# The RMS norms' sums over partitions: one full float32 matmul against two single-pass matmuls of a split operand

## The chip, the core and the metric

The program runs on one core of a Trainium2 chip. A core has five engines with a queue of their own each, worked off in order: TensorE (PE; its weight loads are listed apart as PEld), VectorE (DVE), ScalarE (ACT), GpSimd (POOL) and SyncE (SP), which here issues transfers. The metric is the device time of one execution in microseconds (us). Before the change the median of 3 runs is 1052.08 us (1051.79 to 1053.68).

## What is computed

```
attn = 1 / (1 + exp(-(q k^T / sqrt(D) - log(S))))        # 4 x 12 heads, S = 448, D = 64
x    = attn v, heads side by side                        # 1792 tokens x 768
rms  = sqrt(mean(x * x, axis=-1) + 1e-06)
xn   = x / rms * rms_g
h1   = silu(xn w_gate) * (xn w_val) w_out                # 768 -> 1536 -> 768
out  = ((h1 w1) * (h1 w2)) w3 w_out2                     # 768 -> 1024 -> 1024 -> 768
```

All in float32. The norm needs, for each token, the sum of squares over 768 features.

## The kernel before

Activations lie transposed: features on the 128 partitions, the S = 448 tokens of one batch along the row, so that a 768-wide x is six tiles of 128x448. The four batches b = 0 to 3 are worked off in turn.

Nearly all matmuls take float32 values that were split into two float32r parts, a high part (a copy rounded to float32r, on ScalarE or GpSimd) and a low part (value minus high part, on VectorE or GpSimd); `runs` (L351) multiplies high by high, high by low and low by high, three matmuls of 128x448 for each product. A matmul whose operands are plain float32 is carried out as two passes, which the trace lists as two matmuls of one instruction.

The sums of the norm: `take_out` (L504) squares each of a batch's six attention tiles (L516, L519) and GpSimd adds them up in `acc` (L520). `rms_norm` (L524) multiplies `acc` by a 128x128 tile of ones on TensorE (L529), in plain float32, which leaves the sum over the partitions in every partition of a PSUM tile; ScalarE takes it from there (v, L533), then come the root and its inverse (r, L535 to L544), and `load_x` (L552) multiplies x by r. `rms_norm` is called four times:

- norm 0 inside the attention of batches 0 and 1, between two pairs of heads (about 55 us into the span). VectorE and GpSimd decode and split weights there (`to_float`, L109, and `split_weight`, L132);
- norm 1 while the product of w3 and the last weight matrix is formed (`w3o_groups`, L944; about 99 us), when VectorE and GpSimd also split the x of batch 0;
- norm 2 in the stretch where the gate and value products of batches 0 and 1 (`a_group`, L855) run between the attention pairs of batches 2 and 3 (about 347 us);
- norm 3 after the last pair, between groups of the down product (`b_group`, L885; about 451 us).

From there to the end TensorE forms products of the Winograd kind without norms.

The scheduler of the tile layer sets the order on each engine from the program's order and its own costs, so the place of an instruction in an engine's queue can differ from its place in the code. Scratch tiles of 128x448 rotate through six buffers (`scratch`, L88); PSUM tiles named `psm` rotate through three (L94). Norms 0 and 1 put their sum in a `psm` tile, norms 2 and 3 in a tile `sn` of another pool.

Of the kernel before, what the change touches and what calls it, by code (L numbers as in the profile page):

```python
# [9 lines left out]
F32 = mybir.dt.float32  # L10
F32R = mybir.dt.float32r
U32 = mybir.dt.uint32
AF = mybir.ActivationFunctionType
ALU = mybir.AluOpType
PSUM = bass.MemoryType.PSUM

B, H, S, D = 4, 12, 448, 64
P = 128
# [27 lines left out]
def fused_kernel(ctx: ExitStack, tc: tile.TileContext, qkv, wg, wv, wo, w1, w2, w3, wo2, gam, out):  # L46
    nc = tc.nc

    def pool(name, side=None, space=None):
        kw = {}  # L50
        if side:
            kw["side"] = side
        if space is not None:
            kw["space"] = space
        return tc.alloc_tile_pool(name=name, bufs=1, **kw)

    cst = pool("cst", "left")
    r1a = pool("r1a", "left")
    scr = pool("scr", "left")
# [4 lines left out]
    ps_m = pool("ps_m", space=PSUM)  # L64
# [1 line left out]
    ps_sc = pool("ps_sc", space=PSUM)  # L66
    pools = {}

    ones = cst.tile([P, P], F32, name="ones")
    nc.vector.memset(ones, 1.0)  # L70
    g_sb = cst.tile([P, KD], F32, name="g_sb")
    bias_s = cst.tile([P, 1], F32, name="bias_s")
    nc.vector.memset(bias_s, -math.log(S))
# [5 lines left out]
    w3o = dram.tile([KF2, P, DM], F32, name="w3o")  # L79

    for _ in range(WARM):
        nc.tensor.matmul(ps_m.tile([P, 512], F32, tag="m", bufs=3, name="psm")[:, :P], ones, ones, start=True, stop=True)  # L82

    def parts(pool, tag, bufs, name, w=S, step=0):

# [2 lines left out]
    def scratch(name):  # L88
        return scr.tile([P, S], F32, tag="s", bufs=6, name=name)

    def held(name):
        return scr.tile([P, S], F32, tag="held", bufs=4, name=name)

    def psm():  # L94
        return ps_m.tile([P, 512], F32, tag="m", bufs=3, name="psm")
# [321 lines left out]
    raw, probs, av, acc = {}, {}, {}, {}  # L417
# [106 lines left out]
    def rms_norm(b, log=False):  # L524
        if b < 2:
            ps = psm()[:, :S]
        else:
            ps = ps_sc.tile([P, 2, 512], F32, tag="sc", bufs=2, name="sn")[:, 0, :S]
        nc.tensor.matmul(ps, ones, acc.pop(b), start=True, stop=True)  # L529
        v = scratch("v")  # L530
        r = rms[b] = held("r")
        t = scratch("t")
        nc.scalar.activation(v, ps, AF.Identity, bias=eps_b, scale=1.0 / DM)  # L533
        if log:
            nc.scalar.activation(t, v, AF.Ln)  # L535
            nc.scalar.activation(r, t, AF.Exp, scale=-0.5)
        else:
            nc.scalar.activation(t, v, AF.Sqrt)
            nc.vector.reciprocal(r, t)

        nc.vector.tensor_tensor(out=t, in0=r, in1=r, op=ALU.mult)
        nc.vector.tensor_tensor(out=t, in0=t, in1=v, op=ALU.mult)
        nc.vector.tensor_scalar(out=t, in0=t, scalar1=-0.5, scalar2=1.5, op0=ALU.mult, op1=ALU.add)
        nc.vector.tensor_tensor(out=r, in0=r, in1=t, op=ALU.mult)  # L544
# [355 lines left out]
    def b_units(g):  # L900
        for m in range(KD):
            for b in range(2):
                yield 6.8, (lambda m=m, b=b: b_group(g, m, b)), (i_b2 if g else i_b)[m][1]
# [23 lines left out]
    for i in range(NA + 1):  # L927
        visit(i, (0, NA, 2))
        with tc.issue_after(last_raw[0]):
            if i in DECODE:  # L930
                decode_wo2(DECODE[i])
                load_wo2(DECODE[i] + 2)
            if i in W3_AT:
                W.load_to(W3_AT[i] + 1)
                W.split_to(W3_AT[i] - 1)
        if i == NA - 2:
            load_pair(NA)
        if i == HP + 1:
            rms_norm(0)
        if i > HP + 1:  # L940
            split_x(0, i - HP - 2)
# [10 lines left out]
    split_x(0, KD)  # L952
    w3o_groups(1, (0,))
    rms_norm(1, True)
    w3o_groups(1, (1,))
    for k in range(KD):
# [32 lines left out]
    b = list(b_units(0))  # L989
    beside = a[half_a:] + b[:5]  # L990
    total, spent = sum(u[0] for u in beside), 0.0
    for j, u in enumerate(beside):
        spent += run(u, int(j >= half_a and j % 2 == 1))

        if 1 <= j <= 3:
            for c in ((0, 1), (2,), (3,))[j - 1]:
                scores(first, c)
            visits = list(range(first + 1, NP + 1))
        if j >= split_at and visits and visits[0] < NP and len(raw[visits[0]]) == 2:
            split_keys(visits[0])  # L1000
        while j > 3 and visits and NP + 1 - first - len(visits) < (NP + 1 - first) * (spent - 8.0) / (total - 8.0):
            visit(visits[0], (first, NP, 1))
            split_at = j + 1
            if visits.pop(0) == NA + HP:
                norm_at = j + 1
            if j >= half_a - 1 and visits and visits[0] < NP:
                split_keys(visits[0])
        if j == norm_at:
            rms_norm(2)
# [102 lines left out]
```

## Time and profile before

| | |
|---|---|
| median of 3 runs | 1052.08 us |
| the profiled execution | 1051.55 us |
| its span from first to last instruction | 1049.8 us |
| TensorE busy | 1043.9 us (99%) |
| VectorE busy | 805.5 us (77%) |
| ScalarE busy | 437.3 us (42%) |
| GpSimd busy | 380.6 us (36%) |

The span is the time between the first and the last instruction; 1.75 us of the execution lie around it. Busy shares alone don't tell what bounds a stage: the chain of waits, followed back from the last instruction, and the list of who waited for whom do. The start of a matmul in the trace is where it is issued; its length of some 0.37 us overlaps with that of its neighbours, so a matmul's price in a stream is the distance between starts, or a piece of the chain divided by its count.

### The profile page before, as it was taken

The page shows a single profiled execution, that of the slowest core. Times are in us where ns is not written, and L with a number is a line of the kernel's source. Part 1 is how long each engine was busy: PE and PEld are TensorE (multiplying, and loading weights), DVE is VectorE, ACT ScalarE, POOL GpSimd, SP SyncE. Part 2 cuts the span into 40 slices and gives each one's busy share as a digit, 9 for nine tenths or more (in the row PEclk, how much of TensorE's full clock was granted, in tenths as well). Part 3 has the DMA queues.
Part 4 walks back from the last instruction along what each step waited for, and adds up shares of the span by engine and source line. Part 5 has one row for each costly group of instructions (what it writes and reads, how often), then busy time and mean ns, then how long its engine had stood idle before and what let it go on. Part 6 is the DMA issues. An engine that isn't in the chain of part 4 may idle for free.

```text
span 1049.8 us, 14277 instructions
## 1 busy us (share of the span) xinstructions
PE 1043.9 (99%) x5144; PEld 889.7 (85%) x5144; DVE 805.5 (77%) x1142; ACT 437.3 (42%) x744; POOL 380.6 (36%) x286
## 2 busy tenths in 40 slices
PE   9999999999999999999999999999999999999998
PEld 4338799998777878799999999999999999999997
DVE  5998988878575898789887778973588898577743
ACT  5684332223554653345444444332344454343431
POOL 2656400000212212003555554233555546445552
PEclk9999999999999999999999999999999999999999
DMA  7653555665444577863542113767333455433343
GB/s 262 248 185 104 167 186 176 229 232 207 147 147 147 176 240 268 267 220 133 198 146 72 69 62 106 252 243 258 130 121 121 127 150 179 135 113 110 106 141 100
DMA packets 85990, 175.26 MB, mean 167 GB/s; under 512 B 8480, under 2 KB 56224, under 8 KB 85920
## 3 DMA queue, kind: packets, MB, share of 16 engines
q1 hardware_dynamic: 83040, 170.76, 49.0%
q10 hardware_dynamic: 2880, 3.61, 1.0%
q8 instruction: 40, 0.66, 0.3%
q14 instruction: 30, 0.25, 0.1%
HBM read 127.54 MB, written 46.79 MB: 166 GB/s over the span
## 4 chain that ended last, share of the span: by engine, by line
PE 98%; ACT 1%; POOL 0%; DVE 0%; issue 0%; DVEq 0%; ACTq 0%
PE w L357 40%; PE psm L357 40%; PE av L486 6%; PE psa L357 4%; PE sc L453 4%; PE psm L453 3%; PE av L482 2%; PE psm L82 0%; POOL qk L439 0%; PE sn L529 0%; ACT a L473 0%; ACT qk L438 0%; ACT ws L134 0%; PE psm L529 0%; ACT a L471 0%
## 5 line engine op out<-in xcount | busy, mean ns | idle before, releaser
L357 PE MATMUL w<-w,ws 128*128 128x448 f32 x2052 | 420.5, 366 | 0.0
L357 PEld LDWEIGHTS w<-w,ws 128*128 128x128 f32 x2052 | 385.1, 188 | 33.2 <-DVE v L774 0.4
L138 POOL TENSOR_TENSOR ws<-wf,ws 128x768 fp32r<-128x768 f32 (+1 forms) x79 | 146.8, 1859 | 156.5 <-ACT ws L134 155.5
L357 PE MATMUL psm<-hm,ws 128*128 128x448 f32 x864 | 178.0, 367 | 0.0
L357 PEld LDWEIGHTS psm<-hm,ws 128*128 128x128 f32 x864 | 161.9, 188 | 15.8 <-issue 2.0
L138 POOL TENSOR_TENSOR ws<-wd,ws 128x384 fp32r<-128x384 f32 x100 | 106.7, 1080 | 125.3 <-ACT ws L134 76.4
L134 ACT ACTIVATE ws<-wf 128x768 fp32r<-128x768 f32 (+1 forms) x109 | 90.2, 829 | 138.1 <-PE w L357 36.8
L357 PE MATMUL psm<-x,ws 128*128 128x448 f32 x648 | 136.8, 369 | 0.4 <-DVE s L869 0.4
L357 PEld LDWEIGHTS psm<-x,ws 128*128 128x128 f32 x648 | 120.9, 188 | 15.2 <-issue 4.2
L439 POOL TENSOR_TENSOR qk<-qk 128x960 fp32r<-128x960 f32 x10 | 23.7, 2367 | 176.2 <-ACT qk L438 176.2
L124 DVE SCALAR_TENSOR_TENSOR wf<-wd,wf 128x768 uint32<-128x768 uint32 (+1 forms) x76 | 79.4, 1045 | 2.3
L114 DVE TENSOR_SCALAR mag<-wd 128x768 uint32<-128x768 uint32 (+1 forms) x76 | 45.2, 594 | 46.3 <-DMA wd<-in_wg 16.4
L127 DVE SCALAR_TENSOR_TENSOR wf<-wd,wf 128x768 uint32<-128x768 uint32 (+1 forms) x76 | 72.4, 953 | 1.1
L116 DVE TENSOR_SCALAR wf<-mag 128x768 uint32<-128x768 uint32 (+1 forms) x76 | 60.6, 798 | 14.6 <-POOL ws L138 11.5
L357 PEld LDWEIGHTS psm<-o,ws 128*128 128x128 f32 x384 | 67.3, 188 | 2.4 <-issue 1.7
L357 PE MATMUL psm<-o,ws 128*128 128x384 f32 x384 | 69.3, 339 | 0.0
L134 ACT ACTIVATE ws<-wd 128x384 fp32r<-128x384 f32 x100 | 48.8, 518 | 36.1 <-PE w L357 25.1
L520 POOL TENSOR_TENSOR acc<-acc,sq 128x448 f32<-128x448 f32 x20 | 26.6, 1332 | 94.4 <-ACT sq L519 94.4
L138 POOL TENSOR_TENSOR ws<-s,ws 128x384 fp32r<-128x384 f32 x40 | 42.0, 1049 | 37.1 <-ACT ws L134 37.1
L115 DVE TENSOR_SCALAR mag<-mag 128x768 f32<-128x768 f32 (+1 forms) x76 | 53.9, 709 | 1.7
L774 DVE TENSOR_TENSOR v<-w,u 128x448 f32<-128x448 f32 x34 | 21.0, 618 | 39.2 <-PE w L357 38.8
L473 ACT ACTIVATE a<-sc,bias_s 128x896 f32<-128x896 f32 x48 | 45.5, 995 | 7.8 <-PE sc L453 7.8
(133 smaller groups left out, 1260.6 us busy)
## 6 DMA issues: line engine op xcount, KB each, us to landing
wd<-in_wo SPq DMA_DIRECT2D x20, 768.0 KB, 5.4
wd<-in_w SPq DMA_DIRECT2D x16, 768.0 KB, 4.9
wd<-in_wg SPq DMA_DIRECT2D x12, 768.0 KB, 4.8
wd<-in_wv SPq DMA_DIRECT2D x12, 768.0 KB, 5.2
raw<-in_qkv SPq DMA_DIRECT2D x12, 736.0 KB, 4.1
wd<-in_w SPq DMA_DIRECT2D x16, 512.0 KB, 4.4
w<-wf SPq DMA_DIRECT2D x16, 384.0 KB, 2.6
wd<-w SPq DMA_DIRECT2D x16, 384.0 KB, 3.8
```

The costliest lines, as they stand in the source:

```text
L114: nc.vector.tensor_scalar(out=mag.bitcast(U32), in0=hi, scalar1=0x7FFFFFFF, scalar2=None, op0=ALU.bitwise_and)
L115: nc.vector.tensor_scalar(out=mag, in0=mag, scalar1=HI_MIN, scalar2=HI_MAX, op0=ALU.max, op1=ALU.min)
L116: nc.vector.tensor_scalar(out=u, in0=mag.bitcast(U32), scalar1=3, scalar2=0x3FFFFFFF, op0=ALU.logical_shift_left, op1=ALU.bitwise_and,)
L124: nc.vector.scalar_tensor_tensor(out=u, in0=hi, scalar=0xC0000000, in1=u, op0=ALU.bitwise_and, op1=ALU.bitwise_or)
L127: nc.vector.scalar_tensor_tensor(out=u, in0=lo, scalar=29, in1=u, op0=ALU.logical_shift_right, op1=ALU.bitwise_or)
L134: nc.scalar.activation(t[:, 0, :w], f[:, :w], AF.Copy)
L138: lows.tensor_tensor(out=t[:, 1, :w], in0=f[:, :w], in1=t[:, 0, :w], op=ALU.subtract)
L357: nc.tensor.matmul(ps, w, xt[:, xi, :], start=first and r == 0 and j == 0, stop=last and r == 2 and j == n - 1)
L453: nc.tensor.matmul(o, w[d, k], x[d, q], start=n == 0, stop=n == len(products) - 1)
L473: nc.scalar.activation(a, both, **sigmoid)
L486: nc.tensor.matmul(av[p][d, :], r[:, v + j * D : v + (j + 1) * D], a[:, j, :], start=False, stop=(c == 2))
L520: nc.gpsimd.tensor_tensor(out=acc[b], in0=acc[b], in1=sq, op=ALU.add)
```

## The change

The ones become float32r: a plain float32 tile is filled as before and serves the warming matmuls, and ScalarE copies it to `ones`. In `rms_norm` the sum `acc` is split like other operands: ScalarE writes its high part `nh`, VectorE the low part `nl` = `acc` - `nh`, both in tiles of the scratch rotation, and two single-pass float32r matmuls with the ones add up in one PSUM tile.

```diff
-    ones = cst.tile([P, P], F32, name="ones")
-    nc.vector.memset(ones, 1.0)
+    ones = cst.tile([P, P], F32R, name="ones")
+    plain = scr.tile([P, S], F32, tag="s", bufs=6, name="plain")[:, :P]
+    nc.vector.memset(plain, 1.0)
+    nc.scalar.activation(ones, plain, AF.Copy)
...
-        nc.tensor.matmul(ps_m.tile([P, 512], F32, tag="m", bufs=3, name="psm")[:, :P], ones, ones, start=True, stop=True)
+        nc.tensor.matmul(ps_m.tile([P, 512], F32, tag="m", bufs=3, name="psm")[:, :P], plain, plain, start=True, stop=True)
...
-        nc.tensor.matmul(ps, ones, acc.pop(b), start=True, stop=True)
+        total = acc.pop(b)
+        hi, lo = (scr.tile([P, S], F32R, tag="s", bufs=6, name=n) for n in ("nh", "nl"))
+        nc.scalar.activation(hi, total, AF.Copy)
+        nc.vector.tensor_tensor(out=lo, in0=total, in1=hi, op=ALU.subtract)
+        nc.tensor.matmul(ps, ones, hi, start=True, stop=False)
+        nc.tensor.matmul(ps, ones, lo, start=False, stop=True)
```

Where the new instructions stand in the queues. Rows name the line, the operation, what it writes and reads, and the size; lines of the changed kernel are 2 to 7 higher than those of the kernel before.

VectorE around norm 1, before (xs and x are the scaled x of batch 0 and its low part; mag and wf belong to the decoding of weights):

```order
L114 TENSOR_SCALAR mag<-wd 128x512
L115 TENSOR_SCALAR mag<-mag 128x512
L557 SCALAR_TENSOR_TENSOR xs<-xr,g_sb,r 128x448 x2
L376 TENSOR_TENSOR x<-xs,x 128x448 x2
L116 TENSOR_SCALAR wf<-mag 128x512
```

and in the changed kernel:

```order
L116 TENSOR_SCALAR mag<-wd 128x512
L117 TENSOR_SCALAR mag<-mag 128x512
L564 SCALAR_TENSOR_TENSOR xs<-xr,g_sb,r 128x448 x2
L378 TENSOR_TENSOR x<-xs,x 128x448 x2
L534 TENSOR_TENSOR nl<-acc,nh 128x448
L118 TENSOR_SCALAR wf<-mag 128x512
```

The subtraction stands behind the last two splits of x; on TensorE the norm's two matmuls stand together where the one stood.

TensorE around norm 2, before (qk and v belong to the attention, x and ws to the gate and value products):

```order
L453 MATMUL sc<-qk 128x448 x12
L453 MATMUL psm<-qk 128x448 x6
L357 MATMUL psm<-x,ws 128x448 x18
L529 MATMUL sn<-acc,ones 128x448
L357 MATMUL psm<-x,ws 128x448 x36
L453 MATMUL psm<-qk 128x448 x3
```

and in the changed kernel:

```order
L455 MATMUL psm<-qk 128x448 x6
L359 MATMUL psm<-x,ws 128x448 x31
L535 MATMUL sn<-nh,ones 128x448
L359 MATMUL psm<-x,ws 128x448 x2
L536 MATMUL sn<-nl,ones 128x448
L359 MATMUL psm<-x,ws 128x448 x21
L455 MATMUL psm<-qk 128x448 x3
```

The norm's matmuls moved 13 and 15 matmuls later in the queue.

VectorE at the same place, in the changed kernel (s and hm belong to the gate and value products):

```order
L116 TENSOR_SCALAR mag<-wd 128x768
L117 TENSOR_SCALAR mag<-mag 128x768
L876 TENSOR_TENSOR s<-psm,s 128x448
L378 TENSOR_TENSOR hm<-s,hm 128x448
L534 TENSOR_TENSOR nl<-acc,nh 128x448
L880 TENSOR_TENSOR s<-psm,s 128x448
```

The five other rows stood there in the same order before; the subtraction stands between L378 and L880. At norm 0 it stands on VectorE between a decoded weight's last row (L129) and the next weight's first (L116), and the high part's copy on ScalarE stands between the two activations of the scores `sc`. At norm 3 the low part's matmul stands 10 matmuls later than the norm's stood, and the subtraction behind L117.

## Rows read from the trace of the kernel before

**Rows 1.** The page: busy time of the engines, and the chain that ended last.

```profile
PE 1043.9 (99%) x5144; PEld 889.7 (85%) x5144; DVE 805.5 (77%) x1142; ACT 437.3 (42%) x744; POOL 380.6 (36%) x286
...
PE 98%; ACT 1%; POOL 0%; DVE 0%; issue 0%; DVEq 0%; ACTq 0%
```

**Rows 2.** Who waited for whom, TensorE: us in total, times, longest.

```profile
PE psm L82 <- DVE eps_b L75: 1.1, 1, 1.1
PE psm L453 <- POOL qk L439: 0.5, 1, 0.5
PE psm L357 <- DVE s L869: 0.4, 1, 0.4
PE psm L453 <- ACT a L471: 0.2, 1, 0.2
```

**Rows 3.** Chain in order of time around norms 2 and 1: start, us, what.

```profile
343.23 3.88 PE psm L357 x18
347.10 0.75 PE sn L529 x2
347.86 7.32 PE psm L357 x36
...
99.70 8.42 PE psm L357 x48
```

**Rows 4.** Timeline at norm 0: start, us, engine, line, operation, tiles [idle before <-releaser].

```profile
53.03 0.56 DVE L114 TENSOR_SCALAR mag<-wd 128x768 uint32<-128x768 uint32 x1
...
54.01 1.89 ACT L473 ACTIVATE a<-sc,bias_s 128x896 f32<-128x896 f32 x2
54.35 2.00 POOL L138 TENSOR_TENSOR o<-wf,o 128x768 fp32r<-128x768 f32 x1
54.79 1.98 DVE L116 TENSOR_SCALAR wf<-mag 128x768 uint32<-128x768 uint32 x1
55.79 1.16 ACT L471 ACTIVATE a<-psm,bias_s 128x448 f32<-128x448 f32 x2
56.48 1.02 PE L453 MATMUL psm<-raw 128*128 128x448 f32 x2 [0.19 <-ACT a L471]
58.01 0.95 DVE L127 SCALAR_TENSOR_TENSOR wf<-wd,wf 128x768 uint32<-128x768 uint32 x1
```

**Rows 5.** Timeline at norm 1.

```profile
93.35 1.14 POOL L520 TENSOR_TENSOR acc<-acc,sq 128x448 f32<-128x448 f32 x1
...
98.02 1.89 DVE L376 TENSOR_TENSOR x<-xs,x 128x448 fp32r<-128x448 f32 x2 [0.45 <-POOL x L375]
...
99.52 1.55 POOL L138 TENSOR_TENSOR ws<-wf,ws 128x512 fp32r<-128x512 f32 x1
```

**Rows 6.** Timeline at norm 2.

```profile
347.58 0.57 ACT L371 ACTIVATE hm<-s 128x448 fp32r<-128x448 f32 x1
...
348.05 1.00 ACT L438 ACTIVATE qk<-qk 128x960 fp32r<-128x960 f32 x1
...
349.12 2.26 POOL L439 TENSOR_TENSOR qk<-qk 128x960 fp32r<-128x960 f32 x1 [5.09 <-ACT qk L438]
349.21 2.59 DVE L114 TENSOR_SCALAR mag<-wd 128x768 uint32<-128x768 uint32 x1 [4.36 <-DMA wd<-in_w]
...
352.85 0.61 DVE L376 TENSOR_TENSOR hm<-s,hm 128x448 fp32r<-128x448 f32 x1
```

**Rows 7.** Timeline at norm 3.

```profile
450.96 0.54 ACT L890 ACTIVATE yf<-psm 128x448 f32<-128x448 f32 x1 [2.87 <-PE psm L357]
...
451.93 0.56 DVE L115 TENSOR_SCALAR mag<-mag 128x768 f32<-128x768 f32 x1
```

**Rows 8.** Timeline of eight score matmuls at the start and later.

```profile
4.34 3.06 PE L453 MATMUL sc<-raw 64*128 64x448 f32 x8
...
46.25 1.77 PE L453 MATMUL sc<-raw 64*128 64x448 f32 x8
```

**Rows 9.** Busy time by stretch; the number behind POOL's is the granted clock.

```profile
340.00:360.00 20.00, 20.00 (x110) 15.02 (x108) 15.26 (x18) 12.78 (x19) 3.69 (x2) 1.00 0.51 169
```

## The prediction

> **What bounds the kernel now.** Look first at the busy shares and at the chain that ended last: TensorE is busy 99% of the span and makes up 98% of the chain [rows 1]. A share can deceive, so the next view is who waited for whom. TensorE waited four times for another engine, 2.2 us in all, half of it before its first matmul [rows 2]. Two of those waits, on `L453` for GpSimd and on `L357` for VectorE, end chains that began with a matmul. So a microsecond that TensorE loses anywhere in the attention or the products behind it is not given back later, and one that it saves comes off the end, as long as nothing else becomes late. The chain in order of time gives prices: the norm's float32 matmul takes 0.75 us, a float32r matmul of 128x448 in the stream 7.32 / 36 = 0.203 us [rows 3].
>
> **What is saved.** Each norm's 0.75 us becomes two matmuls of 0.203 us, 0.41 us: 0.34 us saved, 1.36 us for four norms. That is all that the change can bring, 0.13% of the time, under the 0.2% that a measurement of this kernel can tell from no change.
>
> **What is added, and where it stands.** Per norm one copy on ScalarE (0.57 us by the row of `L371`, same size [rows 6]), one subtraction on VectorE (0.61 us by `L376` [rows 6]), and two waits on TensorE: for `nh` and for `nl`. Before, TensorE waited for `acc` alone, which is ready long before it is used (at norm 1, 93.35 + 1.14 = 94.5 against 99.70 - 0.75 = 98.95 [rows 3, 5]). Now the sum goes through VectorE's queue, and TensorE's later matmuls are queued behind its wait. So for each norm the question is when VectorE ends the subtraction and when TensorE comes to it. Times below are those of the trace of before; where TensorE is late by then, the place shifts with it.
>
> The start costs nothing: the extra copy of the ones and a second table load stand on ScalarE, which has no work before the first scores are there, and the warming matmuls wait for the same memset.
>
> *Norm 0.* On ScalarE the copy stands between the two score activations that start at 54.01 (1.89 for both), so it runs from about 54.95 to 55.5. What follows it moves by 0.57 less some overlap: the two `L471` at 55.79. TensorE's next scores at 56.48 waited for the first of these (0.19 idle) because a `psm` bank had to come free [rows 4]; they wait 0.5 us longer. On VectorE the subtraction waits for the copy until 55.5 and then for GpSimd. Rows 4 show why: `L116` takes 1.98 us here where the equal-sized `L114` takes 0.56, since it starts at 54.79, inside GpSimd's `L138` (54.35 to 56.35), and ends 0.42 after it. With VectorE waiting, `L138` should run undisturbed and end a little sooner, near 55.8. Then `nl` is there at 56.3, its matmul is done at 56.5, and the bank at 57.0 remains what ends last: **+0.5 us**; 0.2 if the overlap on ScalarE is larger, 0.9 if `L138` ends as late as before.
>
> VectorE itself falls behind. From `L114` to the `L127` at 58.01 six instructions stand behind the subtraction, three of 0.56, one of two thirds of that, two of 0.95, some 3.95 us now that GpSimd doesn't interrupt them; from 56.3 they end at 60.2 against 58.01 + 0.95 = 58.96: 1.2 us late. VectorE and GpSimd hand work to each other all the way to norm 1 and wait there for no transfer or matmul, so I carry the 1.2 us on, with bounds of 0 and 2.
>
> *Norm 1.* The subtraction stands behind two `L376`, which end at 98.02 + 1.89 = 99.91. By then GpSimd has `L138` waiting (99.52, 1.55 us) and holds VectorE off until 101.07, as at norm 0; 0.48 us later `nl` is ready, at 101.55, and with the lag at 102.75 [rows 5]. With its matmul and the hand-over TensorE goes on at 103.0, where it went on at 99.70 [rows 3]: 3.3 us late, 0.5 of which norm 0 had cost. **+2.8 us.** Without lag and without GpSimd's hold `nl` ends at 99.91 + 0.61 = 100.5 and the norm adds 0.55; with a lag of 2 it adds 3.6. The Trainium skill's page "SBUF — State Buffer", section "Who interferes with whom", says that a VectorE instruction with two SBUF operands and a GpSimd instruction that reads SBUF exclude each other and that the one issued first goes first; the rows of `L116` and `L138` bear it out.
>
> *Norm 2.* TensorE's first 18 matmuls end at 347.11; 13 more at 0.203 bring it to 349.75 [rows 3]. `nh` stands behind `L438` (to 349.05) and is ready at 349.6, in time. Two matmuls later, at 350.4, TensorE wants `nl`. But VectorE begins `L114` only at 349.21, when its weights land, and is held by GpSimd's `L439` (349.12 to 351.38); the three that stand between follow, `L376` ending at 353.46, then the subtraction, at 354.0 [rows 6]. TensorE stands still for 3.7 us. Its last 21 matmuls then run from 354.25 to 358.5, where 36 ended at 347.86 + 7.32 = 355.18. **+3.3 us**, with 2.2 to 3.6 as bounds: 2.2 if the load lands a microsecond earlier and `L114` gets in ahead of GpSimd, 3.6 if the hand-overs are longer. The transfers that change places on SyncE there are needed some ten instructions later, so they cost nothing.
>
> *Norm 3.* GpSimd has no work here. `nh` follows ScalarE's `L890` (to 451.50) and is ready at 452.05, where TensorE, 6 matmuls past 450.86, needs it at 452.1; `nl` follows `L115` (to 452.49) and is ready at 453.05, where four more matmuls bring TensorE to 453.1 [rows 7]. The saving stays, less a hand-over: **-0.3 us**, between -0.34 and +0.5.
>
> *Sum:* 0.5 + 2.8 + 3.3 - 0.3 = +6.3 us. The profiled execution took 1051.55 us (a span of 1049.8 and 1.75 around it); with 6.3 it is 1057.85. The median of the runs, 1052.08, lies 0.5 above it, so the median should become **1058.4 us**. Bounds: 0.2 + 0.55 + 2.2 - 0.34 = +2.6 (1054.7) and 0.9 + 3.6 + 3.6 + 0.5 = +8.6 (1060.7).
>
> **Rivals.**
>
> *The clock falls.* TensorE would stand still for some 3 us at norm 1 and 3.7 at norm 2, longer than anywhere in the trace of before, where its granted clock around norm 2 is 1.00, which is 2.4 GHz [rows 9]. The start shows the price: eight score matmuls at 4.34 take 3.06 us, eight of the same form at 46.25 take 1.77 [rows 8]; TensorE runs at about half pace, 1.2 GHz, from 1.05 until some 7 us, so losing about 3 us. One fall gives +9.3 (1061.4), two +12.3. For: the pause at norm 2. Against: TensorE has full work up to it, and the trace of before has no pause to judge by. The Trainium skill's page "TensorE: Matmul & The Clock Gate", section "HAM oscillation — how this bites in real kernels", tells of a kernel that falls back to the lower clock in its waits for transfers; no run yet shows it here.
>
> *TensorE's lateness is VectorE's gain at norm 2.* If the load that `L114` waits for doesn't depend on TensorE, it lands 3.3 us earlier in relation to it; VectorE is then through before GpSimd's `L439` begins, and norm 2 saves 0.34 instead: 0.5 + 2.8 - 0.34 - 0.3 = +2.7, 1054.8. For: loads run ahead of their use. Against: that load queues on SyncE behind stores that ScalarE's attention results release, which come from TensorE.
>
> *The low part is in time everywhere*, so the result is not slower: VectorE ends the subtraction before TensorE comes, at norm 1 by 99.2 and at norm 2 by 350.4, and at norm 0 ScalarE's overlap hides the copy. Then only the savings are left, -1.36: 1050.7, no change that can be told. For: `acc` is final 4.5 us before norm 1's matmul. Against: the queue places. At norm 1 the instructions ahead of the subtraction end at 99.91 even without any lag, and a queue is worked off in order. A gain of over 0.2% has no source at all.
>
> **How the numbers follow.** Forecast, within its bounds: 0.66. Clock: 0.13. Norm 2 caught up: 0.10, about half of it within 0.2% (which ends at 1054.2). In time everywhere: 0.09. Something else: 0.02. Faster 0.02, same 0.14, slower 0.84. The range takes the forecast's bounds and one fall of the clock: 1054.7 to 1061.4.
>
> **What would show it.** Right: TensorE's waits name `nl` at norms 1 and 2, about 3 and 3.7 us; at norm 0 the wait for `L473`'s bank (`L471` before) grows from 0.2 to about 0.7; at norm 3 there is none or hardly one; the stretch from norm 3 to the end is as long as before. At norm 1 the subtraction itself should show some 1.6 us, most of it GpSimd's hold. Wrong: a norm 2 without a wait, a granted clock under 1.00 behind it, or TensorE waiting elsewhere, for a split of weights that VectorE's lag made late.

## The result: 6.7 us slower, and the profile after

The changed kernel's median is 1058.91 us (6 runs, 1056.68 to 1060.84); the kernel before, run on the same chip, has 1052.19. The ratio is 1.0062, with a 95% interval of 1.0053 to 1.0072: slower, and 0.5 us above the time that was forecast. The profiled execution took 1060.55 us, with a span of 1058.8 where before had 1049.8: 9.0 us more.

The page of the changed kernel, busy time and the chain that ended last, against [rows 1]:

```profile
PE 1047.0 (99%) x5144; PEld 892.1 (84%) x5144; DVE 805.3 (76%) x1146; ACT 441.5 (42%) x750; POOL 379.4 (36%) x286
...
PE 92%; DVE 4%; POOL 2%; DMA 1%; issue 1%; ACT 0%; SPq 0%; DVEq 0%; ACTq 0%; POOLq 0%
```

TensorE's share of busy time is what it was. The chain tells more: 98% TensorE has become 92%, and VectorE and GpSimd, which had almost no part in it, now have 6%. Four norms in 5144 matmuls have tied the end to another engine's queue. The list of who waited for whom says where (us in total, times, longest), against [rows 2]:

```profile
PE sn L536 <- DVE nl L534: 3.6, 1, 3.6
PE psm L536 <- DVE nl L534: 1.7, 1, 1.7
...
PE psm L455 <- ACT a L473: 0.5, 1, 0.5
...
PE av L488 <- ACT a L475: 0.4, 1, 0.4
```

The two longest are new and name `nl`: norm 2 (tile `sn`) and norm 1 (tile `psm`). The third was 0.2, and the last is new; both belong to norm 0. The chain in order of time (start, us, what) at norms 1 and 2, against [rows 3]:

```profile
98.16 1.90 DVE x L378 x2
100.05 1.61 DVE nl L534
...
101.71 0.47 PE psm L536
102.18 9.97 PE psm L359 x48
112.15 1.71 PE sc L455 x8
```

```profile
345.33 0.55 ACT xr L510
346.28 6.91 DMA wd<-in_w
353.21 2.60 DVE mag L116
...
357.38 0.63 DVE nl L534
...
358.06 0.55 PE sn L536
358.61 5.75 PE psm L359 x21
364.36 0.61 PE psm L455 x3
```

Both times the chain reaches TensorE through the subtraction, and through what stands ahead of it on VectorE; at norm 2 that goes back to a load of weights (`wd`) and from there to ScalarE's copy of an attention result (`xr`). At norm 1 TensorE goes on at 102.18 instead of 99.70, 2.5 us late. But there is a second loss: the same 48 matmuls that took 8.42 [rows 3] take 9.97. By the next scores the delay is 112.15 - 108.12 (99.70 + 8.42) = 4.0 us. At norm 2 the attention behind it begins at 364.36, where before it did at 355.18 (347.86 + 7.32 [rows 3]): 9.2 us late, 5.2 of them new. The second loss is the clock that TensorE is granted, which falls from 1.00 to 0.50 for a while (a fall, from here on). Busy time by stretch; the number behind POOL's is the granted clock, the next the DMA share:

```profile
96.00:102.00 6.00, 4.25 (x24) 3.90 (x23) 5.51 (x8) 0.99 (x2) 4.75 (x5) 1.00 0.48 153
102.30:105.70 3.40, 3.40 (x13) 3.40 (x12) 3.26 (x6) 3.35 (x4) 1.25 (x1) 0.50 0.16 58
106.00:110.00 4.00, 4.00 (x25) 4.00 (x24) 2.93 (x3) 1.12 (x3) 3.16 (x4) 1.00 0.85 262
354.00:358.00 4.00, 0.47 (x3) 0.10 (x1) 3.97 (x5) 0.00 (x0) 1.39 (x1) 1.00 0.47 162
358.30:361.70 3.40, 3.40 (x10) 2.99 (x10) 1.12 (x2) 3.01 (x4) 0.00 (x0) 0.50 0.00 0
362.00:366.00 4.00, 4.00 (x19) 2.97 (x19) 3.81 (x4) 2.08 (x5) 0.00 (x0) 1.00 0.00 0
```

In both 0.50 rows TensorE is busy all the time and gets through 10 to 13 matmuls where the 4 us behind them hold 19 to 25. It stood still, the clock was granted at 1.2 GHz for 3.4 us, and then at 2.4 GHz again. Each such stretch costs 1.55 (9.97 - 8.42) to 1.7 us (half of 3.4). Where [rows 9] show 1.00 all through, these two cost 3.3 us together.

So the profiled execution's 9.0 us are: norm 0 +0.8, norm 1 +1.7, norm 2 +3.4, norm 3 -0.2, which is 5.7 us of waits less savings, and 3.3 of clock.

### The profile page after: what moved, and what is told of

It reads as the page before. It is cut to its first block, busy times and chain, and to the rows that moved or that the text cites. A ratio compares the mean times of both kernels' runs of the same rounds, so it can differ in the third digit from the quotient of the medians.

```text
span 1058.8 us, 14278 instructions
## 1 busy us (share of the span) xinstructions
PE 1047.0 (99%) x5144; PEld 892.1 (84%) x5144; DVE 805.3 (76%) x1146; ACT 441.5 (42%) x750; POOL 379.4 (36%) x286
## 4 chain that ended last, share of the span: by engine, by line
PE 92%; DVE 4%; POOL 2%; DMA 1%; issue 1%; ACT 0%; SPq 0%; DVEq 0%; ACTq 0%; POOLq 0%
PE w L359 40%; PE psm L359 38%; PE psa L359 4%; PE av L488 4%; PE sc L455 2%; PE psm L455 2%; PE av L484 1%; DMA wd<-in_w 1%; DVE mag L116 1%; DVE wf L126 1%; DVE x L378 1%; DMA wd<-in_wo 1%; DVE mag L117 1%; DVE wf L129 0%; POOL x L377 0%
## 5 line engine op out<-in xcount | busy, mean ns | idle before, releaser
L140 POOL TENSOR_TENSOR ws<-wf,ws 128x768 fp32r<-128x768 f32 (+1 forms) x79 | 146.0, 1849 | 158.5 <-ACT ws L136 157.5
L140 POOL TENSOR_TENSOR ws<-wd,ws 128x384 fp32r<-128x384 f32 x100 | 106.4, 1076 | 124.2 <-ACT ws L136 114.5
L116 DVE TENSOR_SCALAR mag<-wd 128x768 uint32<-128x768 uint32 (+1 forms) x76 | 48.0, 631 | 43.2 <-DMA wd<-in_wo 15.1
L126 DVE SCALAR_TENSOR_TENSOR wf<-wd,wf 128x768 uint32<-128x768 uint32 (+1 forms) x76 | 78.9, 1038 | 2.3
L129 DVE SCALAR_TENSOR_TENSOR wf<-wd,wf 128x768 uint32<-128x768 uint32 (+1 forms) x76 | 77.4, 1018 | 1.1
L118 DVE TENSOR_SCALAR wf<-mag 128x768 uint32<-128x768 uint32 (+1 forms) x76 | 56.2, 740 | 13.7 <-POOL ws L140 10.8
L140 POOL TENSOR_TENSOR ws<-s,ws 128x384 fp32r<-128x384 f32 x40 | 42.0, 1050 | 37.7 <-ACT ws L136 36.0
L117 DVE TENSOR_SCALAR mag<-mag 128x768 f32<-128x768 f32 (+1 forms) x76 | 50.7, 667 | 1.7
L475 ACT ACTIVATE a<-sc,bias_s 128x896 f32<-128x896 f32 x48 | 45.6, 997 | 6.1 <-PE sc L455 6.0
```

Of the source, the lines that this page charges most:

```text
L116: nc.vector.tensor_scalar(out=mag.bitcast(U32), in0=hi, scalar1=0x7FFFFFFF, scalar2=None, op0=ALU.bitwise_and)
L117: nc.vector.tensor_scalar(out=mag, in0=mag, scalar1=HI_MIN, scalar2=HI_MAX, op0=ALU.max, op1=ALU.min)
L118: nc.vector.tensor_scalar(out=u, in0=mag.bitcast(U32), scalar1=3, scalar2=0x3FFFFFFF, op0=ALU.logical_shift_left, op1=ALU.bitwise_and,)
L126: nc.vector.scalar_tensor_tensor(out=u, in0=hi, scalar=0xC0000000, in1=u, op0=ALU.bitwise_and, op1=ALU.bitwise_or)
L129: nc.vector.scalar_tensor_tensor(out=u, in0=lo, scalar=29, in1=u, op0=ALU.logical_shift_right, op1=ALU.bitwise_or)
L140: lows.tensor_tensor(out=t[:, 1, :w], in0=f[:, :w], in1=t[:, 0, :w], op=ALU.subtract)
```

## The experiments

All kernels ran beside the kernel before, in two groups (medians of before 1051.65 and 1052.13 us). Three theories stood against each other. **The queue place** (theory Q in the expectations): what costs is that the low part stands late in VectorE's queue, behind work that has nothing to do with the norm; the split itself costs nothing. **The split's work** (theory W; in waitonly W is the second matmul alone): the additional instructions, tiles and the second matmul cost by themselves, wherever they stand. **The clock:** the pauses matter mainly by the fall of the clock that follows.

### One norm at a time: only1, only2, only03

The split is made at norm 1 alone, at norm 2 alone, at norms 0 and 3 alone; the other norms multiply in plain float32 as before.

```diff
-        hi, lo = (scr.tile([P, S], F32R, tag="s", bufs=6, name=n) for n in ("nh", "nl"))
+        if b in (1,):        # (2,) in only2, (0, 3) in only03
+            hi, lo = (scr.tile([P, S], F32R, tag="s", bufs=6, name=n) for n in ("nh", "nl"))
...
+        else:
+            nc.tensor.matmul(ps, ones.bitcast(F32), total, start=True, stop=True)
```

> Only norm 1 takes the split sum; norms 0, 2 and 3 multiply the same ones by the plain float32 sum as before. Theory Q (the cost is the queue place of the low part: TensorE waits for a subtraction that stands behind the last two splits of x and behind GpSimd): one wait of TensorE for the low part of about 2.5 us at norm 1, net +2 to +2.5 us over the kernel before, and 1.7 more in those runs in which the granted clock falls behind the wait: 1054.2 to 1056.3. Theory W (the cost is the work that a split adds on ScalarE, VectorE and TensorE, spread evenly): a fourth of the change's +6.7 us, 1053.9, without a wait that stands out.

> Only norm 2 takes the split sum. Theory Q: one wait of TensorE for the low part of about 3.6 us, net +3.4 us, and 1.7 more with a fall of the clock: 1055.6 to 1057.3. Theory W: a fourth of +6.7 us, 1053.9.

> Norms 0 and 3 take the split sum, norms 1 and 2 the plain float32 one. Theory Q: norm 0 costs 0.8 us (ScalarE waits for GpSimd's sum ahead of activations that TensorE needs), norm 3 saves 0.2: +0.6, 1052.8, clock at 1.00. Theory W: half of +6.7 us, 1055.5.

Measured: only1 1054.81 us (ratio 1.0030, 1.0017 to 1.0043), only2 1056.58 (1.0043, 1.0030 to 1.0055), only03 1053.55 (1.0013, 1.0004 to 1.0022). Norm 2 costs most, norm 1 next, and norms 0 and 3 together are no gain. Only1's time alone would fit theory W too (1053.9 lies within its interval); its wait of 4.1 us, below, does not. Only03 lost 1.9 us where theory Q gave it 0.6; its wait at norm 0, below, was longer than the changed kernel's. But 3.2 + 4.9 + 1.9 = 10.0 us, half as much again as all four together (6.7). Two timelines say why (start, us, engine, line, operation, tiles [idle before <-releaser]). Norm 1 of only1, GpSimd, VectorE and TensorE:

```profile
100.21 1.51 POOL L140 TENSOR_TENSOR ws<-wf,ws 128x512 fp32r<-128x512 f32 x1
100.52 1.68 DVE L535 TENSOR_TENSOR nl<-acc,nh 128x448 fp32r<-128x448 f32 x1
102.26 0.47 PE L537 MATMUL psm<-nl,ones 128*128 128x448 f32 x1 [4.10 <-DVE nl L535]
```

and norm 0 of only03:

```profile
50.01 1.45 POOL L522 TENSOR_TENSOR acc<-acc,sq 128x448 f32<-128x448 f32 x1
51.49 0.58 ACT L534 ACTIVATE nh<-acc 128x448 fp32r<-128x448 f32 x1 [3.13 <-POOL acc L522]
51.98 0.99 ACT L475 ACTIVATE a<-sc,bias_s 128x896 f32<-128x896 f32 x1
53.02 0.97 PE L488 MATMUL av<-a,raw 128*64 128x448 f32 x4 [1.72 <-ACT a L475]
```

In only1 TensorE comes to norm 1 undelayed, its `nh` matmul starting at 97.80, waits 4.1 us and gets `nl` at 102.20; in the changed kernel it comes at 99.60, waits 1.7, and gets `nl` at 101.66. (0.9 us of that difference is not norm 0: TensorE's start was faster in only1, with eight scores in 1.77 us where [rows 8] have 3.06.) VectorE and GpSimd reach that point at about the same time whether TensorE is late or not, so lateness from norm 0 is largely given back at norm 1. The prices of norms 0 and 1 can't be added: the scores behind norm 1 start 4.6 us later than before in only1 and 2.1 later in only03, but 4.0 later, not 6.7, in the changed kernel, which splits at both.

In only2 the weights landed 0.7 us earlier than in before, and VectorE's `L116` got in ahead of GpSimd's `qk` (348.98, 2.24 us). That case stood in the forecast as the way to a cheaper norm 2. VectorE and TensorE there:

```profile
348.54 0.56 DVE L116 TENSOR_SCALAR mag<-wd 128x768 uint32<-128x768 uint32 x1 [3.83 <-DMA wd<-in_w]
349.13 2.50 DVE L117 TENSOR_SCALAR mag<-mag 128x768 f32<-128x768 f32 x1
353.29 0.47 PE L537 MATMUL sn<-nl,ones 128*128 128x448 f32 x1 [2.98 <-DVE nl L535]
```

`L116` takes 0.56 instead of 2.59, and the next one, `L117`, 2.50 instead of 0.56: the hold is not avoided, only passed on, and the wait shrinks by no more than the earlier start, from 3.58 to 2.98. The profile of only2 has besides four waits in later products that before doesn't have, 1.2 us in all; its 4.8 us of longer span are not accounted for to the last microsecond.

### The wait without the gain: waitonly

The kernel before, with one VectorE instruction put between `acc` and the float32 matmul: the maximum of `acc` and ScalarE's copy of it, which is `acc` again. Matmuls and ones are those of before.

```diff
-        nc.tensor.matmul(ps, ones, acc.pop(b), start=True, stop=True)
+        total = acc.pop(b)
+        hi, lo = (scr.tile([P, S], F32, tag="s", bufs=6, name=n) for n in ("nh", "nl"))
+        nc.scalar.activation(hi, total, AF.Copy)
+        nc.vector.tensor_tensor(out=lo, in0=total, in1=hi, op=ALU.max)
+        nc.tensor.matmul(ps, ones, lo, start=True, stop=True)
```

> The kernel before, its plain float32 sum over partitions kept, but fed from a copy: ScalarE copies the sum, VectorE takes the greater of the sum and its copy (the same values), and the one float32 matmul reads that. This has the change's wait and its place in VectorE's queue, and none of its savings. Theory Q: the changed kernel's time and the 1.36 us of savings on top, 1059 to 1061, waits for the low part at norms 1 and 2. Theory W (two single-pass matmuls with ones cost more than the rows of other matmuls tell): like the kernel before, 1052 to 1053.

Measured: 1060.93 us (ratio 1.0080, 1.0067 to 1.0093). TensorE's longest waits:

```profile
PE sn L533 <- DVE nl L532: 3.8, 1, 3.8
PE av L486 <- ACT a L473: 1.5, 1, 1.5
PE psm L533 <- DVE nl L532: 1.4, 1, 1.4
```

The same waits at the same places. With no float32r matmul in the norms at all, the kernel is slower by 8.8 us. In the same group of runs the changed kernel is slower by 6.4 (after_again, below). Of the 2.4 between them the matmul time that the split saves makes 1.4; the rest is not accounted for, with four runs against six and falls that differ. In this profile there is no fall behind norm 1, and a single one of twice the length at norm 2:

```profile
356.40:363.10 6.70, 6.10 (x14) 4.80 (x15) 2.75 (x3) 3.78 (x4) 0.00 (x0) 0.50 0.09 33
```

The loss belongs to the way of the sum through the queues of ScalarE and VectorE, not to the split products.

### The same work, earlier in the queues: early123 and pool123

In early123 the split of norms 1 to 3 is written right behind the last addition to `acc`, long before the norm's matmuls; engines and instructions are those of the change. In pool123 GpSimd makes both parts there. Norm 0 stays in plain float32; in the changed kernel its copy already comes so early in ScalarE's queue that it waits for the last addition.

```diff
             nc.gpsimd.tensor_tensor(out=acc[b], in0=acc[b], in1=sq, op=ALU.add)
+            if h == HP - 1 and b:
+                total = acc[b]
+                acc[b] = hi, lo = [scr.tile([P, S], F32R, tag="s", bufs=6, name=n) for n in ("nh", "nl")]
+                nc.scalar.activation(hi, total, AF.Copy)                             # pool123: nc.gpsimd.tensor_copy
+                nc.vector.tensor_tensor(out=lo, in0=total, in1=hi, op=ALU.subtract)  # pool123: nc.gpsimd
```

> Norms 1 to 3 take the split sum, and both halves are made right behind the last addition of the sum in the program, by the same engines with the same instructions; norm 0 keeps the plain float32 matmul. Theory Q: the low part is ready before TensorE comes, no wait for it is left, three times 0.34 us are saved: about 1051.2, clock at 1.00. Theory W: the work is the same as in the changed kernel for three of four norms: three fourths of +6.7, about 1057.

> Norms 1 to 3 take the split sum, with both halves made on GpSimd right behind its last addition of the sum; norm 0 keeps the plain float32 matmul. Theory Q: no wait for the low part, since neither ScalarE's nor VectorE's queue is passed: about 1051, like the version in which ScalarE and VectorE make the halves early. Against it: GpSimd's two instructions (0.6 and 1.1 us) hold VectorE off; if that matters, TensorE waits for a split of weights and the time is 1052 or more.

Measured: early123 1051.09 us (11 runs, ratio 0.9993, 0.9984 to 1.0002), pool123 1052.34 (11 runs, 1.0002, 0.9993 to 1.0011). All of TensorE's waits in early123, and VectorE and TensorE at its norm 2:

```profile
PE psm L84 <- DVE eps_b L77: 1.1, 1, 1.1
PE psm L455 <- POOL qk L441: 0.5, 1, 0.5
PE psm L359 <- DVE s L881: 0.4, 1, 0.4
PE psm L455 <- ACT a L473: 0.2, 1, 0.2
```

```profile
344.69 0.61 DVE L527 TENSOR_TENSOR nl<-acc,nh 128x448 fp32r<-128x448 f32 x1
...
346.86 0.36 PE L538 MATMUL sn<-nh,ones 128*128 128x448 f32 x1
...
347.06 0.36 PE L539 MATMUL sn<-nl,ones 128*128 128x448 f32 x1
```

These are the four waits of [rows 2] again. `nl` is ready at 345.30, 1.8 us before its matmul; the norm's matmuls are back behind 18 others, as before the change, and start 0.20 apart. The span is 1049.0 against 1049.8: three times 0.34 saved makes 1.0. That is under what the runs can tell, and the interval of the ratio includes 1. The profile of pool123 has the same four waits, and its 1052.34 is no loss that can be told from none. This settles the theories for norms 1 to 3: the same instructions on the same engines at another place in the queue cost nothing that can be measured, so the split's work falls as a cause, and the queue place stands. Early123 is the best version found, and it is not measurably better than the kernel before.

### Work for TensorE in the pauses: fill

Between the high and the low part's matmul, 14 small matmuls at norm 1 and 36 at norm 2 go into unused columns of the same PSUM bank, so that TensorE doesn't stand still while it waits (`bank` is the whole PSUM tile, `ps` its first 448 columns). The rest is the changed kernel.

```diff
         nc.tensor.matmul(ps, ones, hi, start=True, stop=False)
+        for _ in range({1: 14, 2: 36}.get(b, 0)):
+            nc.tensor.matmul(bank[:, S:], ones, hi[:, : 512 - S], start=False, stop=False)
         nc.tensor.matmul(ps, ones, lo, start=False, stop=True)
```

> The changed kernel with more work for TensorE in its two long waits: between the high and the low part's matmul stand 14 (norm 1) and 36 (norm 2) matmuls of the ones with 64 columns of the high part, into columns of the PSUM bank that nobody reads. If the pauses make the granted clock fall, and the fall costs 1.7 us each time (3.4 us at half pace): clock 1.00 in every run, the added matmuls hide in the waits, about 1057, with less spread than the changed kernel's. If the clock has another cause: falls as before and about the changed kernel's time, 1058.5 to 1061.

Measured: 1059.3 us (5 runs, ratio 1.0071, 1.0058 to 1.0083): no gain. In its profile no wait names `nl`, so the fillers did cover the pauses, and there is no fall at norm 1. At norm 2 there is one all the same. TensorE there, and busy time by stretch:

```profile
351.99 4.14 PE L538 MATMUL sn<-nh,ones 128*128 128x64 f32 x36
355.94 0.72 PE L539 MATMUL sn<-nl,ones 128*128 128x448 f32 x1
```

```profile
352.00:355.80 3.80, 3.80 (x36) 3.80 (x35) 3.79 (x4) 0.00 (x0) 1.78 (x1) 1.00 0.42 126
355.95:359.30 3.35, 3.35 (x11) 3.00 (x11) 0.66 (x2) 2.55 (x4) 0.00 (x0) 0.50 0.15 58
```

A stretch with a listed busy share of 1 is followed by a fall as well. The mean granted clock says how long a run was at the lower level: 0.998 is 3.4 us at half clock in some 1058, one fall of that length, and 1.000 is none. Two of the five runs have 0.998, none has less; in the two sets of runs of the changed kernel nine of twelve have 0.998 or less. So falls were rarer in these five runs, and not ended. The time did not follow, and why is not shown: in this profile TensorE is 1.7 us ahead of the changed kernel's first profile behind norm 2 (362.45 against 364.19, in spite of a wait for `L475` at norm 0 of 1.5 us instead of 0.4), and 0.8 ahead at the end, but the medians, 1059.3 and 1058.5, lie the other way and within each other's play. As a test of the clock theory the run is inconclusive.

### The changed kernel again: after_again

The same kernel a second time, on the chip of the second group.

> The changed kernel once more, on the chip of the other runs, to compare with them: 1058.5 (1056.5 to 1061), and the runs with a mean granted clock of 1.00 some 1.7 us faster for each fall than those with 0.998 or less.

Measured: 1058.53 us (6 runs, 1054.89 to 1060.84; ratio 1.0059, 1.0043 to 1.0075). Its profile has the waits again, 3.6 and 1.9 us, and both falls. Together with the first set there are twelve runs, which sort themselves by their mean granted clock (the last column is against 1052.15, about the median of before in both sets):

| mean granted clock | runs | mean time, us | above before, us |
|---|---|---|---|
| 1.000 (none at 0.50) | 3 | 1057.0 | 4.8 |
| 0.998 (3.4 us) | 4 | 1058.1 | 5.9 |
| 0.996, 0.997 (about 7 us) | 5 | 1060.3 | 8.1 |

The lowest group is two falls in the two profiles, but waitonly's 0.997 is a single long one, so for the other runs the number of falls is not known. From the first group to the last the time grows by 3.3 us, about 1.65 for each 3.4 us at half clock, the size that the profile gave. The groups are small, and only2 doesn't follow them: its one run at 1.000 took 1057.03, its four at 0.998 took 1055.5 to 1057.6. Without a fall the change still costs 4.8 us, by three runs that lie between 1054.9 and 1059.4. So the clock makes the loss larger, but does not make it.

## Why the prediction was right, and where its steps were not

The time (1058.4 forecast, 1058.9 measured) and the sign held. The mechanism held: nothing is gained beyond 0.34 us per norm, and the new wait for the subtraction behind unrelated work on VectorE costs more. early123 and waitonly show it from both sides. That the number came so close is partly luck: VectorE's lag and with it norm 1 were too large in the sum, and the clock, which the sum left out, came in.

**Saved, 1.36 us.** Right as far as it can be told: three norms without waits gave 0.8 us of span where 1.0 was worked out. The plain float32 matmul's 0.75 us are 3.7 float32r matmuls, though the trace lists it as two: "two passes" counts its rows and does not give its price.

**Norm 0, +0.5 forecast, +0.8 measured, by another mechanism.** The step "on ScalarE the copy stands between the two score activations that start at 54.01" named the wrong pair. `nh` stands one pair of heads earlier. Timeline of the changed kernel, against [rows 4]:

```profile
48.71 1.44 POOL L522 TENSOR_TENSOR acc<-acc,sq 128x448 f32<-128x448 f32 x1
50.18 0.58 ACT L533 ACTIVATE nh<-acc 128x448 fp32r<-128x448 f32 x1 [1.86 <-POOL acc L522]
50.66 0.99 ACT L475 ACTIVATE a<-sc,bias_s 128x896 f32<-128x896 f32 x1
...
51.71 1.72 PE L488 MATMUL av<-a,raw 128*64 128x448 f32 x7 [0.45 <-ACT a L475]
...
52.47 0.62 DVE L534 TENSOR_TENSOR nl<-acc,nh 128x448 fp32r<-128x448 f32 x1
```

There the copy waits for GpSimd's last addition, ScalarE stands for 1.86 us, and the activation queued behind it is what TensorE's `av` needs. From the first of these `av` matmuls to the next scores it takes 3.37 us (50.29 to 53.66), before 2.40 (50.41 to 52.81); the longer wait for `L473`, 0.5 instead of 0.2, uses up norm 0's saving. Not the 0.57 us of the copy is the price but its wait, and the wait depends on when GpSimd gets there and when TensorE does: addition done at 50.15 in this profile, a TensorE wait of 0.4; at 51.46 in only03, as in before (49.85 + 1.45 = 51.30), a wait of 1.7; at 50.25 in fill, where TensorE was 1.0 us earlier, 1.5. The forecast's range for norm 0, 0.2 to 0.9, covered the first and not the second.

**VectorE's lag, 1.2 us forecast, 0.1 measured, of 0.7 that the subtraction caused.** "The subtraction waits for the copy until 55.5 and then for GpSimd" falls with the wrong place: `nh` was there before VectorE came, and the subtraction took 0.62 with nothing holding it. The instruction that ended at 58.96 before [rows 4] (`L127`, now `L129`) ends at 59.08, by its piece of the chain:

```profile
58.21 0.87 DVE wf L129
```

But VectorE was 0.6 us ahead here: the `L129` in front of the subtraction starts at 51.59, the same row of the kernel before (`L127`) at 52.16. From that start to the same end it takes 7.5 us instead of 6.8. In only03 VectorE was not ahead (52.31), the row ends at 59.78, 0.8 late, and the last `L378` before norm 1 at 100.75 instead of 99.91. So a lag that is carried on to norm 1 was right in kind; its size is 0.7, and in the changed kernel's profile a lead whose cause was not looked for hid most of it.

**Norm 1, +2.8 forecast, +1.7 measured.** The mis-sized term is that lag. The rest of the step held: VectorE ends the last `L378` at 100.05 (99.91 before), GpSimd's `L140` runs from 99.66 to 101.17, and the subtraction took 1.68 us under its hold, for which 1.6 was forecast. Set the lag to 0.1 and the forecast is 1.7; that it meets the measured 1.7 is partly luck, since TensorE then goes on at 101.9 instead of 102.18, and norm 0 had cost 0.8 of that and not 0.5. The Trainium skill, "SBUF — State Buffer", section "Who interferes with whom", says that of a GpSimd instruction and a VectorE instruction that contend the one issued first has the shared ports to its end. These rows agree, 1.68 us against 0.62 for the same subtraction at norm 0, and so do the 2.59 us of `L116` at norm 2 and the 2.50 of `L117` in only2, where 0.56 is the undisturbed time. The prediction named the rows of `L116` and `L138` of the kernel before for instructions with two operands; that `L116` reads one tensor, so those rows showed a hold but not that case, which the subtraction shows.

**Norm 2, +3.3 forecast, +3.4 measured.** Each step can be read in the trace, moved by the 4.0 us that TensorE was late: VectorE gets its weights at 353.2 (349.2 before [rows 6]), `L116` takes 2.59 beside GpSimd's `qk`, `L117`, `L876` and `L378` follow, `nl` at 357.38. The rival by which the load would land earlier in relation to TensorE falls with the first of these. What the prediction held against it is what happened: the load is issued right behind the store of an attention result, at 342.25 before and at 346.28 now, so it shifts with TensorE's lateness. The lower bound of 2.2 would not have come true even in only2, where VectorE was first: the attention behind norm 2 begins 2.9 us late there.

**Norm 3, -0.3 forecast, -0.2 measured.** The low part is in time, and no wait is listed:

```profile
461.56 0.62 DVE L534 TENSOR_TENSOR nl<-acc,nh 128x448 fp32r<-128x448 f32 x1
...
462.32 0.39 PE L536 MATMUL sn<-nl,ones 128*128 128x448 f32 x1
```

**The clock, a rival with a chance of 0.13, and 3 us for each fall.** The chance was too low and the price too high. Time at the lower clock shows in nine of twelve runs, and 3.4 us of it cost 1.65. The price was taken from the start, where half pace lasts for 6 us; in the profiles of the changed kernel it lasted 3.4 behind a pause (6.7 in waitonly). The start was a poor measure in another way too: the profile lists a granted clock of 1.00 there, so that the half pace is known from the matmuls alone, and the same eight scores take 1.77 us in the profiles of only1 and fill. And the rival was set up as an alternative to the forecast, though nothing in it excluded the forecast's waits: it should have been an addition to them. The Trainium skill's page "TensorE: Matmul & The Clock Gate", section "HAM oscillation — how this bites in real kernels", tells of a kernel that falls to the lower clock in its waits for transfers, and this trace agrees for waits on VectorE of 1.75 and 3.58 us.

Put together: leaving out the clock, 5.7 us in the profile and 4.8 in the runs, where 6.3 was forecast, and on top of it 1.65 to 3.3 from the clock in those runs that had a fall.

## What to carry to other kernels

When an operand's preparation goes to another engine, its price is not its duration but the work that stands ahead of it in that engine's queue, and whatever is queued behind its own wait: look up both in the order before counting what the faster instruction saves. If the source is final long before its use, as `acc` was here by 2.9 us or more, write the preparation close behind the source; at norms 1 to 3 the same instructions then cost nothing that can be measured. Norm 0 shows the limit: its copy stood so close behind the source that ScalarE waited 1.86 us for it, and with it the activation that TensorE needed. Whether a later place would have made norm 0 free was not tried. And a saving of 0.34 us per use, four times in 1052 us, can't pay for a single wait like those of norm 1 or 2.

## What the runs showed of the hardware

A single pause of TensorE of 1.75 us, in a stretch that it had filled without a gap, was followed by 3.4 us at half clock, which cost about as much again as the pause. The pause is not the whole story. In the profile of only2 TensorE stood for 2.98 us and the clock stayed at 1.00:

```profile
350.00:354.00 4.00, 1.02 (x5) 0.67 (x4) 3.23 (x4) 0.21 (x1) 1.22 (x1) 1.00 0.45 148
354.00:358.00 4.00, 4.00 (x21) 3.69 (x20) 2.27 (x2) 3.57 (x4) 0.00 (x0) 1.00 0.02 7
```

while the clock in fill fell with no pause listed. In waitonly a pause of 1.42 us at norm 1 was not followed by a fall, and at norm 2 the clock fell 0.6 us before a pause of 3.75 us ended and stayed down for 6.7. What decides whether a given pause is followed by a fall stays open.

The work of VectorE and GpSimd at norm 0 comes up to 1.3 us earlier or later from one kernel to the next (the last addition ends at 50.15 in after, 51.46 in only03) although VectorE and GpSimd work off the same instructions in the same order ahead of it. That is enough to move TensorE's wait there from 0.4 to 1.7 us, so a price read from one execution's timeline has that much play. What shifts the two engines was not tried.
